# An operation planner on one core: GpSimd left out of the shared work in the first third of the plan, and one weight load moved behind the attention inputs

## The chip, the core and the metric

The kernel runs on one core of a Trainium2 chip. It has the engines TensorE (PE, with its weight loads PEld), VectorE (DVE), ScalarE (ACT), GpSimd (POOL) and SyncE (SP, which here issues the transfers). The metric is the time of one execution on the device in microseconds, as a median of runs. The profile is of one further execution, whose own time stands beside its span below.

## The reference, cut to what matters

Three layers one after the other, on inputs of float32, with weights that arrive as float64 words:

```
for c in range(24):                       # linear attention, chunks of 32 positions
    cum = cumsum(log_a[chunk]);  L = exp(cum_i - cum_j) * causal
    y[chunk] = (C B^T * L) x  +  (C state) * exp(cum)
    state = exp(sum(log_a)) * state + sum_j(B_j x_j * exp(cum_last - cum_j))
xk = mu_k*x + (1-mu_k)*x_prev;  xr = mu_r*x + (1-mu_r)*x_prev     # channel mix
x  = sigmoid(xr @ w_r) * (relu(xk @ w_k)**2 @ w_v)               # 256 -> 1024 -> 256
h  = max(x @ w1, x @ w2, x @ w3);  out = h @ w_out               # 256 -> 768 -> 256
```

Batch 4, 8 heads, 768 positions, head size 32, state 16; 3072 tokens in all.

## The kernel before

The 3072 tokens go through in six tiles t = 0 to 5 of 512 tokens. For each tile the attention makes decay masks, the products of C and B, the chunk states and y; then come the mix, the gate (xr @ w_r), the two feed-forward products and the three-way maximum.

Each float32 operand of a product is split into a high and a low part (names ending in h and l): a copy makes the high part (L414 on ScalarE, L416 on VectorE), and `sub` at L422 subtracts it to leave the low part. A product is then three matmuls (high by high, low by high, high by low). So wkl, wrl, wvl, xk00l, k2l are low parts.

Each weight is loaded by `load_split`: one transfer brings the float64 words as pairs of 32-bit words into a staging buffer (h_93, h_94, woh ...); ScalarE takes the absolute value of the upper words (L630), VectorE turns them into float32 in four steps (L631, L633, L635, L637), and then the copy and the subtraction follow. w_k's first half is loaded in two parts, c = 0 and c = 1 (L659 to L661).

In the attention of a tile, `bd` (L764) is the scaled B for the state update, `sbd` the state (L788 scales it, L790 adds the update `um`), `ce` (L848) the scaled C. TensorE makes the products of C and B in two banks pb (L860), VectorE multiplies them with the masks L (L872), TensorE makes y out of it (L895), which is copied to xb (L933). The mix is L965 to L968, the gate L986, the first feed-forward product L1011 in eight groups f, whose results ScalarE takes out of the banks pa (L1017 ReLU, L1018 square); L1020 and L1021 are the square once more, for the low part.

No order is written by hand. Class `Plan` collects each operation with a cost for each engine that can run it, and a list scheduler places them all, 60 times over with improved keys; the order of the best plan is the order in which the instructions are put onto the engines. An operation that has a cost for "DVE" and one for "POOL" goes to the engine that is free first, in the plan's time (`now`, in ns). In `forward` GpSimd leaves such an operation alone only if VectorE is free or has other work that needs the port which the two engines share in the plan. A key is lowered by the operation's bias; a transfer's bias is `first` plus the plan's bias of the moment. `AHEAD[0]` is the bias of the mix for the feed-forward of tile 0, `AHEAD[1]` the bias in force while w_k's first half is declared, and `FIRST` the bias of the first transfers (b_t 9.85e5, x 9.8e5, c_w 9.9e5, w_r 9.83e5, w_k 9.5e5, mus 9.95e5, c_t 9.6e5; b_t and c_w carry C and B of tile 0).

Of the kernel before, what the change touches and what calls it, by code (L numbers as in the profile page):

```python
# [25 lines left out]
class Ring:  # L26
# [6 lines left out]
    def next(self):  # L33
        b = self.bufs[self.i % len(self.bufs)]
        self.i += 1
        return b
# [39 lines left out]
class Plan:  # L76
# [14 lines left out]
    FIRST = 1500.0  # L91
# [5 lines left out]
    WARM = (3400.0, 430.0, 215.0, 100.0, 200.0)  # L97
    EARLY = 104
    ROUNDS = 60
    SPARE = (200.0, 1000.0)  # L100
    ENGINES = ("PE", "ACT", "POOL", "DVE", "SP")

# [35 lines left out]
    def forward(self, key, spare):  # L138
# [36 lines left out]
        while done < n:  # L175
            now = heapq.heappop(events)
# [15 lines left out]
            for e in self.ENGINES:  # L192
# [12 lines left out]
                if e == "POOL":  # L205
                    if "DVE" in ops[i][0]:
                        mine = next((k for k in sorted(q) if where[k[1]] is None and "DVE" not in ops[k[1]][0]), None)
                        wanted = free["DVE"] <= now or any(
                            ops[k[1]][8] and k[1] != i and where[k[1]] is None for k in ready["DVE"])
                        if wanted:  # L210
                            if mine is None:
                                if free["DVE"] > now:
                                    heapq.heappush(events, free["DVE"] + 1.0)
                                continue
                            q.remove(mine)
                            heapq.heapify(q)
                            heapq.heappush(q, (q[0][0] - 1.0 if q else mine[0], mine[1]))
                elif e == "DVE" and port > now and ops[i][8]:
                    other = min((k for k in q if not ops[k[1]][8] and where[k[1]] is None), default=None)
                    if other is not None:  # L220
                        q.remove(other)
                        heapq.heapify(q)
                        heapq.heappush(q, (q[0][0] - 1.0, other[1]))
# [70 lines left out]
    def arrange(self):  # L294
# [11 lines left out]
        best = None  # L306
        for k in range(self.ROUNDS):
            start, end, where = self.forward(key, self.SPARE[k % len(self.SPARE)])
            if best is None or max(end) < best[0]:
# [27 lines left out]
SPREAD = 2  # L337
LATE = 0
EARLY1 = -20000.0
AHEAD = (60000.0, 60000.0)  # L340
FIRST = (9.85e5, 9.8e5, 9.9e5, 9.83e5, 9.5e5, 9.95e5, 9.6e5)


# [1 line left out]
def kernel(  # L345
# [24 lines left out]
    FF = w_k.shape[1]  # L370
# [74 lines left out]
    b_wk = [[Buf(), Buf()] for _ in range(KC)]  # L445
# [199 lines left out]
    def weights_front():  # L645
        plan.bias = BIAS[2]
        dma(100, mu.rearrange("p i c -> p (i c)"), mus, w=[b_mu], first=FIRST[5])
        op("DVE", 100, lambda: V.tensor_scalar(
            out=om, in0=mu, scalar1=-1.0, scalar2=1.0, op0=ALU.mult, op1=ALU.add), r=[b_mu], w=[b_om])
        fs = [slice(0, FF // 2), slice(FF // 2, FF)]  # L650
        wide, narrow = [Buf(), Buf()], [Buf(), Buf()]
        b_pre.extend(wide[:1] + narrow[:1])
        plan.bias = BIAS[1]
        load_split(w_r.rearrange("p (k n) -> p k n", k=KC), wr_t[0], wr_t[1], KC, CH, [b_wr], FIRST[3],
                   place=(stage.next(2 * TW), word.next(TW)))
        plan.bias = AHEAD[1]
        spots = [(stage.next(2 * TW), word.next(TW)), ((wo_f[0][:, :2 * TW], wide[:1]), word.next(TW)),
                 (stage.next(4 * TW), (wo_f[1][:, :2 * TW], narrow[:1]))]
        for c in range(KC):  # L659
            load_split(w_k[c * P:(c + 1) * P, None, fs[0]], wk_t[0][:, c:c + 1, fs[0]], wk_t[1][:, c:c + 1, fs[0]],  # L660
                       1, FF // 2, [b_wk[c][0]], FIRST[4] - 1.5e5 * c, place=spots[c])  # L661
        plan.bias = 0.0
        k = [begun['loads']]
        load_split(w_k[:, fs[1]].rearrange("(c p) n -> p c n", p=P), wk_t[0][:, :, fs[1]], wk_t[1][:, :, fs[1]],
                       KC, FF // 2, [b_wk[c][1] for c in range(KC)], FIRST[4] - 4e5, place=spots[2], after=k)
        inputs(1, (FIRST[4] - 4.2e5, FIRST[4] - 4.3e5), after=k)
        dma(935, bt.rearrange("p u i -> p (u i)"), b_t[1], w=[b_bt], first=FIRST[4] - 4.4e5, after=k)
        dma(1870, cw.rearrange("p u i -> p (u i)"), c_w[1], w=[b_cw], first=FIRST[4] - 4.5e5, after=k)
        dma(935, ct.rearrange("p u i -> p (u i)"), c_t[1], w=[b_ct], first=FIRST[4] - 2e5)
        for f in range(FC // 4):  # L670
            load_split(w_v[f].rearrange("p (k n) -> p k n", k=4), wv_t[0][:, 4 * f:4 * f + 4], wv_t[1][:, 4 * f:4 * f + 4], 4, CH, [b_wv[f]])
# [323 lines left out]
    def ffn(half, t):  # L995
        hv, cols, bs, n = tokens(half)
        xkt, b_xkt = xk_hl[t % 2], b_xk[t % 2]
        plan.bias += AHEAD[0] * (t == 0)
        mix(0, xkt, b_xkt, half, t)
        plan.bias -= AHEAD[0] * (t == 0)  # L1000

# [125 lines left out]
    plan.switch = begun['spread'], begun['carried']  # L1127
    plan.bias = 0.0
    weights_front()
    sums()  # L1130
    weights_back()
# [93 lines left out]
```

## Time and profile before

| what | value |
| --- | --- |
| time, median of 3 runs | 407.53 us (407.53 to 408.23) |
| time of the profiled execution | 408.05 us |
| its span | 406.3 us |
| PE busy | 396.3 us, 98% |
| DVE busy | 257.9 us, 63% |
| ACT busy | 216.1 us, 53% |
| POOL busy | 55.0 us, 14% |
| granted TensorE clock | 0.9 or more in all 40 slices |

The span runs from the first to the last instruction of the profiled execution. The difference of 1.75 us between its time and its span is start and end around it. Busy shares are over the whole span; what limits a stretch has to be read from that stretch.

### The profile page before, as it was taken

How to read it: one execution, taken by the hardware profiler on the slowest of the kernel's cores; microseconds unless marked ns; L12 is line 12 of the kernel's file. 1: busy time of each engine (PE TensorE's matmuls, PEld its weight loads, DVE VectorE, ACT ScalarE, POOL GpSimd, SP SyncE). 2: the span in 40 equal slices, each digit the busy share in tenths (PEclk: the TensorE clock that was granted, in tenths of full speed). 3: DMA queues.
4: the chain of work that ended last, by engine and by line, in shares of the span. 5: the costliest groups of instructions: out<-in, count | busy, mean ns of one | idle time of the engine just before them, and what ended most of it. 6: DMA issues, size and time to landing. Idle time of an engine off the chain costs nothing.

```text
span 406.3 us, 8667 instructions
## 1 busy us (share of the span) xinstructions
PE 396.3 (98%) x3684; PEld 318.0 (78%) x3684; DVE 257.9 (63%) x417; ACT 216.1 (53%) x379; POOL 55.0 (14%) x60
## 2 busy tenths in 40 slices
PE   8789999999999999999999999999999999999996
PEld 5557877788877888888888888888787888888885
DVE  5898999999998945573735473755373315430632
ACT  6489878954767743355743255753246733321321
POOL 5121000000004100421400231320022200010010
PEclk9999999999999999999999999999999999999999
DMA  7596559541335200206100002300000000001001
GB/s 251 187 369 193 180 139 259 164 141 33 129 112 152 73 26 0 71 38 177 31 27 0 28 2 66 66 26 0 2 2 27 0 26 2 0 0 54 0 2 52
DMA packets 12879, 31.55 MB, mean 78 GB/s; under 512 B 1768, under 2 KB 4136, under 8 KB 12072
## 3 DMA queue, kind: packets, MB, share of 16 engines
q1 hardware_dynamic: 12840, 30.99, 24.7%
q8 instruction: 29, 0.48, 0.5%
q14 instruction: 10, 0.08, 0.1%
HBM read 27.64 MB, written 3.34 MB: 76 GB/s over the span
## 4 chain that ended last, share of the span: by engine, by line
PE 80%; DVE 13%; issue 2%; DMA 2%; ACT 2%; SPq 0%; DVEq 0%; ACTq 0%
PE pa L689 32%; PE pa L1032 14%; PE pa L1011 13%; PE pa L1108 9%; PE pa L986 3%; PE pb L1108 2%; DVE L L872 2%; DVE tmp L1070 1%; PE pb L895 1%; DMA h<-in_w_k_dram 1%; PE pb L860 1%; DVE k2l L422 1%; DMA outs<-in_w_out_dram 1%; DVE tmp L968 1%; DVE h L637 1%
## 5 line engine op out<-in xcount | busy, mean ns | idle before, releaser
L1070 DVE TENSOR_TENSOR tmp<-tmp,pa 128x512 f32<-128x512 f32 x72 | 49.0, 684 | 55.3 <-PE pa L689 54.5
L422 DVE TENSOR_TENSOR k2l<-tmp,k2h 128x512 fp32r<-128x512 f32 x53 | 39.9, 764 | 40.9 <-ACT tmp L1020 34.0
L414 ACT ACTIVATE hr<-tmp 128x512 fp32r<-128x512 f32 x35 | 22.1, 632 | 69.3 <-DVE tmp L1070 69.1
L1032 PE MATMUL pa<-k2h,wvh 128*128 128x512 f32 x96 | 38.2, 398 | 0.0
L1032 PE MATMUL pa<-k2h,wvl 128*128 128x512 f32 x96 | 38.0, 395 | 0.0
L1032 PE MATMUL pa<-k2l,wvh 128*128 128x512 f32 x96 | 37.8, 393 | 0.0
L1108 PE MATMUL pa<-hr,worh 128*128 128x512 f32 x120 | 37.4, 393 | 0.0
L1017 ACT ACTIVATE tmp<-pa 128x512 f32<-128x512 f32 x48 | 28.3, 590 | 10.3 <-PE pa L1011 8.6
L1068 ACT ACTIVATE tmp<-pa 128x512 f32<-128x512 f32 x36 | 21.5, 598 | 21.8 <-PE pa L689 20.2
L1018 ACT ACTIVATE k2h<-tmp 128x512 fp32r<-128x512 f32 x48 | 30.2, 631 | 2.6 <-PE pa L1032 1.0
L422 DVE TENSOR_TENSOR hr<-tmp,hr 128x512 fp32r<-128x512 f32 x28 | 19.5, 700 | 14.8 <-ACT hr L414 14.7
L1108 PEld LDWEIGHTS pa<-hr,worh 128*128 128x128 f32 x120 | 22.3, 188 | 5.3 <-ACT th L991 0.7
L422 POOL TENSOR_TENSOR hr<-tmp,hr 128x512 fp32r<-128x512 f32 x8 | 10.3, 1292 | 110.8 <-ACT hr L414 110.8
L1020 ACT ACTIVATE tmp<-tmp 128x512 f32<-128x512 f32 x37 | 23.2, 630 | 0.8
L1108 PE MATMUL pa<-hr,worl 128*128 128x512 f32 x60 | 23.4, 389 | 0.0
L1032 PEld LDWEIGHTS pa<-k2h,wvh 128*128 128x128 f32 x96 | 18.0, 188 | 4.4 <-ACT k2h L414 0.2
L1032 PEld LDWEIGHTS pa<-k2h,wvl 128*128 128x128 f32 x96 | 18.0, 188 | 4.4
L1032 PEld LDWEIGHTS pa<-k2l,wvh 128*128 128x128 f32 x96 | 18.0, 188 | 4.1
L790 POOL TENSOR_TENSOR sbd<-sbd,um 128x256 f32<-128x256 f32 x2 | 3.1, 1548 | 117.8 <-DVE sbd L788 117.8
L1079 ACT ACTIVATE outs<-pa 128x512 f32<-128x512 f32 x9 | 5.4, 600 | 25.5 <-PE pa L1108 25.5
L968 DVE SCALAR_TENSOR_TENSOR tmp<-xb,bits,tmp 128x512 f32<-128x512 f32 x24 | 17.2, 745 | 0.3
L872 DVE TENSOR_TENSOR L<-pb,L 128x512 f32<-128x512 f32 (+1 forms) x28 | 15.7, 603 | 1.6 <-PE pb L860 0.8
(273 smaller groups left out, 977.4 us busy)
## 6 DMA issues: line engine op xcount, KB each, us to landing
h<-in_w_dram SPq DMA_DIRECT2D x6, 768.0 KB, 5.0
L<-crd SPq DMA_DIRECT2D x8, 512.0 KB, 6.9
cw<-in_c_w_dram SPq DMA_DIRECT2D x6, 512.0 KB, 4.5
xt<-in_x_l_dram SPq DMA_DIRECT2D x6, 512.0 KB, 7.8
out_dram<-outs SPq DMA_DIRECT2D x10, 256.0 KB, 2.0
h<-in_w_v_dram SPq DMA_DIRECT2D x2, 1024.0 KB, 7.6
bt<-in_b_t_dram SPq DMA_DIRECT2D x6, 256.0 KB, 4.7
bl<-in_b_l_dram SPq DMA_DIRECT2D x6, 256.0 KB, 6.5
```

The source lines that it names most:

```text
L414: A.activation(ap(out_), ap(in_), AF.Copy)
L422: op({"DVE": tt(n), "POOL": pool(n, narrow)}, 0, lambda e: (V if e == "DVE" else G).tensor_sub(ap(out_), ap(x0), ap(x1)), r=r, w=w, after= ...
L689: T.matmul(pt, l, r_, start=(i == 0), stop=(i == last))
L872: op("DVE", tt(2 * step * HP), lambda q=q, b=b, lq=lq: V.tensor_mul(lq, W[q].ap[:, b * P:(b + step) * P].rearrange("p (b r i) -> p r b i", ...
L1011: T.matmul(p.ap[:, :n], l, r_, start=(c == 0 and i == 0), stop=(c == KC - 1 and i == 2))
L1017: op("ACT", 51 + 0.833 * n, lambda: A.activation(sq, p.ap[:, :n], AF.Relu), r=[p], w=[tm])
L1018: op("ACT", act(n), lambda: A.activation(hi, sq, AF.Square), r=[tm], w=[kb])
L1020: A.activation(sq, sq, AF.Square) if e == "ACT" else
L1032: T.matmul(pv[c2].ap[:, :n], l, r_, start=(f == 0 and i == 0), stop=(f == FC - 1 and i == 2))
L1068: op("ACT", 51 + 0.833 * TW, lambda p=p, tm=tm: A.activation(tm.ap, p.ap, AF.Copy), r=[p], w=[tm])
L1070: op("DVE", tt(TW), lambda p=p, tm=tm: V.tensor_tensor(out=tm.ap, in0=tm.ap, in1=p.ap, op=ALU.max), r=[p], w=[tm])
L1108: T.matmul(p.ap, l, r_, start=(g == 0 and i == 0), stop=(g == GC - 1 and i == 2))
```

## The change

A class constant `QUIET` of 140000 (plan ns) is added. As long as the plan's time is below it, GpSimd takes no operation that VectorE could run too; it takes one that only it or another engine can run, or nothing. `AHEAD` goes from 60000 to 20000 in both entries: the mix of tile 0 and the steps of w_k's first half get less bias. The transfer of w_k's first half has `AHEAD[1]` taken off its own `first`, so that its whole bias goes from 1.01e6 to 9.5e5 for c = 0, and from 8.6e5 to 8.0e5 for c = 1.

```diff
--- before.py
+++ after.py
@@ -97,6 +97,7 @@
     WARM = (3400.0, 430.0, 215.0, 100.0, 200.0)
     EARLY = 104
     ROUNDS = 60
+    QUIET = 140000.0
     SPARE = (200.0, 1000.0)
     ENGINES = ("PE", "ACT", "POOL", "DVE", "SP")
 
@@ -207,7 +208,7 @@
                         mine = next((k for k in sorted(q) if where[k[1]] is None and "DVE" not in ops[k[1]][0]), None)
                         wanted = free["DVE"] <= now or any(
                             ops[k[1]][8] and k[1] != i and where[k[1]] is None for k in ready["DVE"])
-                        if wanted:
+                        if wanted or now < self.QUIET:
                             if mine is None:
                                 if free["DVE"] > now:
                                     heapq.heappush(events, free["DVE"] + 1.0)
@@ -337,7 +338,7 @@
 SPREAD = 2
 LATE = 0
 EARLY1 = -20000.0
-AHEAD = (60000.0, 60000.0)
+AHEAD = (20000.0, 20000.0)
 FIRST = (9.85e5, 9.8e5, 9.9e5, 9.83e5, 9.5e5, 9.95e5, 9.6e5)
 
 
@@ -658,7 +659,7 @@
                  (stage.next(4 * TW), (wo_f[1][:, :2 * TW], narrow[:1]))]
         for c in range(KC):
             load_split(w_k[c * P:(c + 1) * P, None, fs[0]], wk_t[0][:, c:c + 1, fs[0]], wk_t[1][:, c:c + 1, fs[0]],
-                       1, FF // 2, [b_wk[c][0]], FIRST[4] - 1.5e5 * c, place=spots[c])
+                       1, FF // 2, [b_wk[c][0]], FIRST[4] - AHEAD[1] - 1.5e5 * c, place=spots[c])
         plan.bias = 0.0
         k = [begun['loads']]
         load_split(w_k[:, fs[1]].rearrange("(c p) n -> p c n", p=P), wk_t[0][:, :, fs[1]], wk_t[1][:, :, fs[1]],
```

The line numbers of the changed kernel are one higher from L100 on.

**The transfers at the start.** SyncE issues the transfers in this order behind those of la and mus (h_94 is a staging buffer; `128x1024` is 512 KB, `128x512` 256 KB). Before:

```order
L427 DMA h_94<-in_w_k_dram 128x1024
L427 DMA cw<-in_c_w_dram 128x1024
L427 DMA bt<-in_b_t_dram 128x512
L427 DMA bl<-in_b_l_dram 128x512
L427 DMA h_94<-in_w_r_dram 128x1024
L427 DMA xt_121<-in_x_l_dram 128x1024
```

After:

```order
L428 DMA cw<-in_c_w_dram 128x1024
L428 DMA bt<-in_b_t_dram 128x512
L428 DMA bl<-in_b_l_dram 128x512
L428 DMA h_94<-in_w_r_dram 128x1024
L428 DMA xt_121<-in_x_l_dram 128x1024
L428 DMA ct<-in_c_t_dram 128x512
L428 DMA h_94<-in_w_k_dram 128x1024
L428 DMA woh<-in_w_k_dram 128x1024
```

The transfer of w_k's first part has moved from the third place behind that of ct; cw, bt, bl and w_r each stand 512 KB earlier.

**VectorE at the start.** It begins the weights and the first tile's masks so (rows behind lal, the low part of the log decays; h_92 is the float32 word buffer). Before, w_k's steps, then the eight products with the masks in four lines:

```order
L631 TENSOR_SCALAR h_92<-h_92 128x512
L633 TENSOR_SCALAR h_92<-h_92 128x512
L635 SCALAR_TENSOR_TENSOR h_92<-h_94,h_92 128x512
L598 CAST tri<-h_91 128x128
L637 SCALAR_TENSOR_TENSOR h_92<-h_94,h_92 128x512
L422 TENSOR_TENSOR wkl<-h_92,wkh 128x512
L872 TENSOR_TENSOR L<-pb_135,L 128x2x128 x2
L872 TENSOR_TENSOR L<-pb_136,L 128x2x128 x2
L872 TENSOR_TENSOR L<-pb_135,L 128x2x128 x2
L872 TENSOR_TENSOR L<-pb_136,L 128x2x128 x2
```

After, bd first, and the steps of w_r with its low part among and behind the eight products:

```order
L765 TENSOR_TENSOR bd<-bl,dfj 128x512
L873 TENSOR_TENSOR L<-pb_135,L 128x2x128 x2
L873 TENSOR_TENSOR L<-pb_136,L 128x2x128 x2
L632 TENSOR_SCALAR h_92<-h_92 128x512
L634 TENSOR_SCALAR h_92<-h_92 128x512
L636 SCALAR_TENSOR_TENSOR h_92<-h_94,h_92 128x512
L873 TENSOR_TENSOR L<-pb_135,L 128x2x128 x2
L873 TENSOR_TENSOR L<-pb_136,L 128x2x128 x2
L638 SCALAR_TENSOR_TENSOR h_92<-h_94,h_92 128x512
L632 TENSOR_SCALAR h_92<-h_92 128x512
L634 TENSOR_SCALAR h_92<-h_92 128x512
L423 TENSOR_TENSOR wrl<-h_92,wrh 128x512
```

The steps of w_k come behind those of w_r, and its low part wkl, which stood ahead of the eight products, comes eight rows after this piece.

**GpSimd behind its set-up.** L573 is the last of the constants. Before:

```order
L573 TENSOR_TENSOR bits<-um 128x2
L764 TENSOR_TENSOR bd<-bl,dfj 128x512
L788 TENSOR_TENSOR sbd<-sbd,ec 128x256
L422 TENSOR_TENSOR wrl<-h_92,wrh 128x512
L764 TENSOR_TENSOR bd<-bl,dfj 128x512
L422 TENSOR_TENSOR k2l_100<-tmp_107,k2h_99 128x512
L790 TENSOR_TENSOR sbd<-sbd,um 128x256
L1021 TENSOR_TENSOR tmp_110<-tmp_110 128x512
L1021 TENSOR_TENSOR tmp_107<-tmp_107 128x512
L422 TENSOR_TENSOR L<-L,ccol 128x512
L790 TENSOR_TENSOR sbd<-sbd,um 128x256
```

After:

```order
L574 TENSOR_TENSOR bits<-um 128x2
L791 TENSOR_TENSOR sbd<-sbd,um 128x256
L849 TENSOR_TENSOR ce<-ct,ec 128x512
L423 TENSOR_TENSOR hr_1444<-tmp_109,hr_1444 128x512
L928 COPY xb_129<-xb_130 128x8
```

Nine operations are gone from GpSimd here, among them L788 sbd and the two L1021. VectorE goes from 399 to 406 rows (ScalarE and VectorE also exchange some).

**ScalarE at w_v.** The rows around the second half of w_v (wd<-h_93 is its absolute value, wvh the high part of the first half; pa_131 and pa_132 are TensorE's banks). Before:

```order
L1018 ACTIVATE k2h_103<-tmp_109 128x512
L1020 ACTIVATE tmp_109<-tmp_109 128x512
L1017 ACTIVATE tmp_110<-pa_132 128x512
L414 ACTIVATE wvh<-h_92 128x1024
L1017 ACTIVATE tmp_107<-pa_131 128x512
L1018 ACTIVATE k2h_105<-tmp_110 128x512
L630 ACTIVATE wd<-h_93 128x1024
```

After:

```order
L1021 ACTIVATE tmp_109<-tmp_109 128x512
L1018 ACTIVATE tmp_110<-pa_132 128x512
L631 ACTIVATE wd<-h_93 128x1024
L415 ACTIVATE wvh<-h_92 128x1024
L1018 ACTIVATE tmp_107<-pa_131 128x512
L1019 ACTIVATE k2h_105<-tmp_110 128x512
L1021 ACTIVATE tmp_110<-tmp_110 128x512
```

The absolute value of w_v's second half has moved ahead of wvh, and so ahead of the ReLU that empties the bank pa_131.

## Rows read from the trace of the kernel before

**Rows 1.** Busy time of each engine in two stretches (us; clock, DMA share, GB/s last)

```profile
24.00:64.00 40.00, 39.09 (x600) 30.04 (x600) 38.66 (x54) 33.40 (x61) 3.25 (x2) 1.00 0.66 212
64.00:126.00 62.00, 61.55 (x625) 49.35 (x625) 61.51 (x113) 43.30 (x81) 0.00 (x0) 1.00 0.43 125
```

**Rows 2.** What TensorE waited for after 24 us (total, times, longest)

```profile
PE pb L727 <- issue: 1.5, 1, 1.5
PE pa L1011 <- ACT tmp L1017: 0.8, 1, 0.8
PE pa L1011 <- DVE outs L1081: 0.4, 1, 0.4
```

**Rows 3.** The end of the chain of waits from 36 to 64 us

```profile
62.41 0.61 DVE xk00l L422
...
63.75 0.50 PE pa L1011
```

**Rows 4.** GpSimd's timeline, 9 to 36 us (start, duration, what)

```profile
9.79 1.06 POOL L764 TENSOR_TENSOR bd<-bl,dfj 128x512 f32<-128x512 f32 x1 [3.23 <-DMA bl<-in_b_l_dram]
...
19.61 1.27 POOL L422 TENSOR_TENSOR wrl<-h,wrh 128x512 fp32r<-128x512 f32 x1 [4.06 <-ACT wrh L414]
24.24 1.53 POOL L764 TENSOR_TENSOR bd<-bl,dfj 128x512 f32<-128x512 f32 x1 [3.36 <-DMA bl<-in_b_l_dram]
32.90 1.73 POOL L422 TENSOR_TENSOR k2l<-tmp,k2h 128x512 fp32r<-128x512 f32 x1 [7.13 <-DVE wol L635]
```

**Rows 5.** VectorE's timeline, 0 to 70 us

```profile
6.91 0.43 DVE L631 TENSOR_SCALAR h<-h 128x512 f32<-128x512 f32 x1 [0.41 <-ACT h L630]
...
7.83 0.69 DVE L635 SCALAR_TENSOR_TENSOR h<-h,h 128x512 uint32<-128x512 uint32 x1
...
9.96 1.44 DVE L422 TENSOR_TENSOR wkl<-h,wkh 128x512 fp32r<-128x512 f32 x1 [0.70 <-ACT wkh L414]
...
12.55 2.08 DVE L872 TENSOR_TENSOR L<-pb,L 128x256 f32<-128x256 f32 x6 [0.82 <-PE pb L860]
15.45 0.42 DVE L872 TENSOR_TENSOR L<-pb,L 128x256 f32<-128x256 f32 x1 [0.82 <-PE pb L895]
...
19.99 1.44 DVE L637 SCALAR_TENSOR_TENSOR wd<-woh,wd 128x512 uint32<-128x512 uint32 x1
...
24.16 2.16 DVE L422 TENSOR_TENSOR k2l<-tmp,k2h 128x512 fp32r<-128x512 f32 x2 [0.34 <-ACT k2h L414]
...
31.05 0.69 DVE L631 TENSOR_SCALAR h<-h 128x1024 f32<-128x1024 f32 x1 [0.60 <-ACT h L630]
...
33.40 2.32 DVE L637 SCALAR_TENSOR_TENSOR wol<-h,wol 128x1024 uint32<-128x1024 uint32 x1
...
37.73 1.22 DVE L422 TENSOR_TENSOR wkl<-wol,wkh 128x1024 fp32r<-128x1024 f32 x1 [0.55 <-ACT wkh L414]
...
55.10 1.28 DVE L422 TENSOR_TENSOR k2l<-tmp,k2h 128x512 fp32r<-128x512 f32 x2
```

**Rows 6.** ScalarE's timeline, 0 to 45 us

```profile
10.92 0.67 ACT L630 ACTIVATE h<-h 128x512 f32<-128x512 f32 x1 [0.51 <-DMA h<-in_w_r_dram]
...
41.22 0.59 ACT L1017 ACTIVATE tmp<-pa 128x512 f32<-128x512 f32 x1
...
42.21 1.15 ACT L630 ACTIVATE wd<-h 128x1024 f32<-128x1024 f32 x1
```

**Rows 7.** TensorE's timeline, 0 to 45 us

```profile
9.13 0.70 PE L860 MATMUL pb<-cw,bt 32*64 32x128 f32 x32 [0.56 <-DMA bt<-in_b_t_dram]
...
26.15 0.58 PE L986 MATMUL pa<-k2h,wrh 128*128 128x512 f32 x1
```

**Rows 8.** Issues of w_v's two halves (KB, us from issue to landing)

```profile
h<-in_w_v_dram SPq DMA_DIRECT2D x1, 1024.0 KB, 10.4
...
h<-in_w_v_dram SPq DMA_DIRECT2D x1, 1024.0 KB, 4.9
```

**Rows 9.** Busy time in the first stretch after 126 us

```profile
126.00:140.00 14.00, 14.00 (x61) 11.43 (x62) 12.17 (x22) 11.57 (x22) 5.62 (x4) 1.00 0.59 151
```

## The prediction

> **What bounds the kernel now.** I read the busy times by stretch first, since the shares over the whole span hide the stages. From 24 to 64 us VectorE is busy 38.66 of 40 us and TensorE 39.09; from 64 to 126 us it is 61.51 and 61.55 of 62 [rows 1]. Two engines are full at once, so the waits have to say which one leads. Behind 24 us TensorE waits for anything but its own queue in only three places: 1.5 us for its own issue (while it makes the second tile's masks), 0.8 us for a ReLU of ScalarE, and 0.4 us for an eviction by VectorE [rows 2]. The chain followed back from that ReLU ends in xk00l, a low part that VectorE has done at 63.0 us, and TensorE goes on at 63.75 [rows 3]; the steps ahead of it on that chain are nearly all VectorE's. So up to 63 us VectorE's queue decides when TensorE goes on, and behind it TensorE runs to the end without a gap except for the 0.4 us. What the change is worth is what it does to the time at which VectorE ends xk00l, plus that 0.4 us. I place three landmarks on VectorE: the last of the eight products with the masks ends at 15.87 us (15.45 + 0.42), the second low part of the gate's operand ends at 26.32 (24.16 + 2.16), xk00l at 63.0 [rows 3, 5]. The gate's first matmul starts at 26.15, within the second of these [rows 7].
>
> **GpSimd's operations, taken back.** The early five are bd, sbd, wrl, bd, k2l. An operation with two operands costs VectorE one step of 0.60 us at 512 elements (two of them take 1.28 us, where one shows 0.69) and about 0.34 at 256 (six take 2.08, one 0.42) [rows 5]. So they cost it 4 x 0.60 + 0.34 = 2.74 us. But they held it up where they were. Each long VectorE row here began while a GpSimd row ran, and ended about 0.6 us (1.2 at 1024 elements) after that one's end: wkl 1.44 us from 9.96 beside bd 9.79 to 10.85; L637 1.44 from 19.99 beside wrl 19.61 to 20.88; two k2l 2.16 from 24.16 beside bd 24.24 to 25.77; L637 2.32 from 33.40 beside k2l 32.90 to 34.63 [rows 4, 5]. Against 0.69, 0.69, 1.28 and 1.22 without company [rows 5] that is 0.75 + 0.75 + 0.88 + 1.10 = 3.48 us of standstill. Taken back, the five are therefore worth only 0.7 us in VectorE's favour; the rest of the gain has to come from the order.
>
> The Trainium skill, SBUF — State Buffer, section "Who interferes with whom", says that VectorE and GpSimd share a port pair under an exclusive lock, held for the whole instruction, the loser standing fully blocked, also for a VectorE operation with two SBUF inputs against a GpSimd one that reads SBUF. The rows agree: wkl ends 0.55 us after bd, as if it had started there. By that rule the four standstills go in full; by a rule of shared bandwidth part of them would stay, but the rows show no such part.
>
> **The front, up to 15.87 us.** The transfers land in the order of issue: bl at 9.79 (GpSimd was waiting for it), w_r at 10.92 (ScalarE was) [rows 4, 6]. In the new order the same bytes stand ahead of and in w_r as now in and ahead of bl (512 + 256 + 256 KB, and w_r's 512 in place of w_k's). So w_r should land near 9.7. ScalarE's step takes 0.67, so 10.35; VectorE's three steps 1.61 (from 6.91 to 8.52) [rows 5], so 11.95; the last four products with the masks stand behind them, 4 x 0.34, so 13.3. The bank they read has been made by then: the first products of C and B started at 9.13, waiting for bt [rows 7], which comes 512 KB earlier. bd is VectorE's first such step (0.60) and hides in the wait for w_r. If w_r lands no earlier than now, it is 10.92 + 0.67 + 1.61 + 1.36 = 14.55; if nothing in the front comes earlier, 15.87.
>
> **From there to the gate.** Now 26.32 − 15.87 = 10.45 us. Two standstills lie in it and go (0.75 + 0.88). Work changes: the four steps of w_k, wrl and wkl come in (0.34 + 0.34 + 4 x 0.60 = 3.08), three steps of w_r and one of w_k's second part go out (0.34 + 0.34 + 2 x 0.60 = 1.88): +1.20. This gives 10.0 and a landmark of 23.3 (24.6 and 25.9 for the two worse fronts). TensorE could start its gate earlier than that, so it is again VectorE that it meets.
>
> **From the gate to xk00l.** Now 63.0 − 26.3 = 36.7 us. The standstill of 1.10 goes. VectorE gets more in this piece: L637 that moved behind (0.60), sbd (0.34), a copy to the high part and a masked update from ScalarE (0.34 each), bd and k2l (0.60 each), a weight's low part of 768 elements drawn ahead of xk00l (0.87, priced by the difference of the 512 and 1024 steps), less a copy that went to ScalarE (0.60): +3.09. One idle time of 0.60, in which VectorE waits for ScalarE's step on w_v's first half at 31.05 [rows 5], goes at least in part because VectorE now comes to it later in its own list: that half took 10.4 us to land [rows 8], and its issue hangs on buffers that come free earlier, not later. I take it as gone; the other idle time of 0.55 at 37.73 I leave, since its cause is ScalarE's order. So 36.7 − 1.1 + 3.1 − 0.6 = 38.1, and xk00l is done at 61.4. TensorE follows 0.75 behind, as now: 62.15 against 63.75, −1.6 us. With 24.6 it is −0.3, with 25.9 it is +1.0.
>
> **Behind it.** The low part of 0.87 us is no longer in the 62 us that follow, and the eviction that TensorE waits for (0.4) goes to ScalarE: −0.4 us, with nothing as the other bound. The last four of the nine operations (sbd and three of 0.60, 2.1 us) come to VectorE behind 126 us, where it is busy 12.17 of 14 us [rows 9] in the fullest stretch, and TensorE does not wait. I cost them at nothing; were the cover gone, 0.6 us for each that stands at the head of a wait.
>
> **The sum.** −1.6 − 0.4 = −2.0 us on the profiled 408.05, 406.05. The median of the runs lies 0.5 below the profiled time, so 405.5. About 0.2%, 0.8 us, is what a measurement of this kernel can tell from no change.
>
> **The rivals.** (1) The front gains little: w_r lands no earlier than now, because the transfers share what the memory gives rather than their order. Then −0.3 and −0.4 give 406.8; if the front gains nothing at all +1.0 − 0.4 gives 408.1. For it speaks that the landing times above are worked out, not seen; against it that bt, bl and w_r landed in order and that engines waited for two of them [rows 4, 7].
>
> (2) Slower: w_v's second half lands late. Its absolute value (1.15 us, now at 42.21) stands ahead of wvh and of the ReLU that empties pa_131 (now 41.22 to 41.81) [rows 6]. ScalarE takes its list in order, so the ReLU waits for the transfer, and TensorE for the bank. The transfer can be issued when VectorE has read the buffer with L637 (33.40, end 35.72), in the new order near 31.6. With the 4.9 us that it took [rows 8] it lands at 36.5 and costs nothing. It decides from 40.9 on. With the 10.4 us of the first half it lands at 42.0, the ReLU ends at 42.0 + 1.15 + 1.05 (wvh) + 0.6 = 44.8, 3.0 us later than now; less the 0.8 that TensorE waits later anyway, and the 0.4: +1.8, so 409.3. For it speaks that the same size did take 10.4 us once, against it that the queue was then behind much else.
>
> (3) More gain: the idle time of 0.55 goes as well, and the front gains the 0.6 us by which the landings are uncertain. xk00l at 60.2, then −2.8 − 0.4 gives 404.3.
>
> (4) GpSimd's work runs beside VectorE's almost freely, the long rows being late for other reasons. Then three of the standstills that I take off behind the front (0.75 + 0.88 + 1.10 = 2.73 us) stay: 405.5 + 2.7 gives 408.2. The rows speak against it, four times out of four. The Trainium skill, Perfetto Trace Analysis, section "Optimizing Scalar/DVE Operations", says that with VectorE saturated some of its work may well go to GpSimd, which speaks against this change, and adds that the shared port may undo it.
>
> **How the numbers follow.** My forecast 0.52, with 404.6 to 406.5 of its own; rival 1 0.20, rival 2 0.12, rival 3 0.12, rival 4 0.04. Faster by over 0.2% are the forecast and rival 3: 0.64. Within it rivals 1 and 4: 0.24. Slower rival 2: 0.12. The range goes from rival 3's lower side, 404.0, to rival 4 and the worse half of rival 1, 408.2; it leaves out rival 2.
>
> **What the new profile would show.** Right: no GpSimd row with two operands ahead of 126 us, and no subtraction of 512 elements on VectorE above 0.7 us nor one of 1024 above 1.25; the last product with the masks ends near 13.3, the gate's second low part near 23.3, xk00l near 61.4; TensorE restarts near 62.2 and shows short waits between 23 and 62 us that add up to two or three, since its work from the gate on is less than VectorE's. The step that fails is the front if w_r's absolute value starts at 10.9 or behind, the piece from the gate if VectorE shows idle times for ScalarE's copies, and rival 2 if VectorE is well ahead while the ReLU behind w_v's absolute value ends behind 42 us. The prediction is wrong if VectorE is done at 61.4 and TensorE still goes on at 63.75, since something else then holds it.

## The result: slower by 0.6 per cent, and the profile after

The changed kernel takes 410.63 us as a median of 20 runs (407.3 to 413.5), the kernel before 407.53 (20 runs, 407.1 to 410.0): a ratio of 1.0058, 95% interval 1.0037 to 1.0078. A second set gave 410.22 against 407.91, again 1.0058 (1.0032 to 1.0085). I had forecast 405.5. The profiled execution took 411.31 us with a span of 409.6, 3.3 more than before.

Busy time by stretch, as in [rows 1] (the columns are PE, PEld, DVE, ACT, POOL, the granted clock, DMA share, GB/s):

```profile
0.00:24.00 24.00, 20.59 (x502) 13.91 (x502) 17.30 (x40) 15.34 (x31) 4.68 (x24) 1.00 0.62 220
24.00:64.00 40.00, 36.07 (x569) 27.70 (x570) 38.39 (x59) 30.44 (x53) 0.00 (x0) 1.00 0.70 229
64.00:126.00 62.00, 60.02 (x617) 48.00 (x616) 59.70 (x108) 44.54 (x83) 0.00 (x0) 1.00 0.41 121
```

The kernel before, up to 24 us:

```profile
0.00:24.00 24.00, 18.80 (x479) 13.11 (x480) 17.94 (x38) 15.44 (x28) 8.34 (x27) 1.00 0.69 243
```

Up to 24 us TensorE is busy 20.59 us, 1.8 more than the 18.80 of before: the front did gain. From 24 to 64 it loses 3.0 (36.07 against 39.09), from 64 to 126 another 1.5. What it waited for behind 24 us, to be held against [rows 2]:

```profile
PE pa L1012 <- ACT tmp L1018: 4.3, 3, 2.3
PE pa L1012 <- DVE wkl L423: 0.7, 1, 0.7
PE pb L896 <- issue: 0.7, 1, 0.7
PE pa L987 <- DVE k2l L423: 0.5, 1, 0.5
```

4.3 us are for ReLUs of ScalarE (L1018 here is L1017 of before), in three pieces. ScalarE's timeline at the two large ones answers to [rows 6]:

```profile
38.39 0.61 ACT L1018 ACTIVATE tmp<-pa 128x512 f32<-128x512 f32 x1
41.05 1.12 ACT L631 ACTIVATE wd<-h 128x1024 f32<-128x1024 f32 x1 [2.05 <-DMA h<-in_w_v_dram]
42.06 1.05 ACT L415 ACTIVATE wvh<-h 128x1024 fp32r<-128x1024 f32 x1
43.01 0.59 ACT L1018 ACTIVATE tmp<-pa 128x512 f32<-128x512 f32 x1
...
65.09 0.89 ACT L631 ACTIVATE h<-h 128x768 f32<-128x768 f32 x1 [3.77 <-DMA h<-in_w_dram]
65.88 0.62 ACT L415 ACTIVATE xk01h<-tmp 128x512 fp32r<-128x512 f32 x1
66.40 0.58 ACT L1018 ACTIVATE tmp<-pa 128x512 f32<-128x512 f32 x1
```

At the first place ScalarE is idle 2.05 us for the landing of w_v's second half, and the ReLU of group 4 stands two rows behind the waiting one, at 43.01 (41.22 before). At the second it is idle 3.77 us for the next weight (768 columns), and behind that row stand xk01h and the second tile's first ReLU, at 66.40. Before, the same row stood behind the second tile's first two ReLUs (L1017) and found the weight landed:

```profile
63.10 0.60 ACT L1017 ACTIVATE tmp<-pa 128x512 f32<-128x512 f32 x1 [0.50 <-DVE xk00l L422]
...
64.26 0.58 ACT L1017 ACTIVATE tmp<-pa 128x512 f32<-128x512 f32 x1
64.93 0.92 ACT L630 ACTIVATE h<-h 128x768 f32<-128x768 f32 x1
```

In the changed kernel TensorE starts again right behind each of the two late ReLUs:

```profile
43.65 0.50 PE L1012 MATMUL pa<-xk00h,wkh 128*128 128x512 f32 x1 [2.31 <-ACT tmp L1018]
...
67.03 0.50 PE L1012 MATMUL pa<-xk10h,wkh 128*128 128x512 f32 x1 [1.82 <-ACT tmp L1018]
```

67.03 is the start that stood at 63.75 before [rows 3]: 3.28 us later, as much as the span grew. VectorE, answering to [rows 5]:

```profile
9.44 0.69 DVE L765 TENSOR_TENSOR bd<-bl,dfj 128x512 f32<-128x512 f32 x1 [2.58 <-DMA bl<-in_b_l_dram]
...
14.14 1.09 DVE L873 TENSOR_TENSOR L<-pb,L 128x256 f32<-128x256 f32 x3 [0.82 <-PE pb L896]
...
20.55 0.68 DVE L423 TENSOR_TENSOR wkl<-h,wkh 128x512 fp32r<-128x512 f32 x1
...
23.53 1.28 DVE L423 TENSOR_TENSOR k2l<-tmp,k2h 128x512 fp32r<-128x512 f32 x2
...
42.20 0.69 DVE L632 TENSOR_SCALAR wd<-wd 128x1024 f32<-128x1024 f32 x1 [1.14 <-ACT wd L631]
...
63.23 0.69 DVE L423 TENSOR_TENSOR xk00l<-tmp,xk00h 128x512 fp32r<-128x512 f32 x1
...
66.53 0.69 DVE L423 TENSOR_TENSOR xk01l<-tmp,xk01h 128x512 fp32r<-128x512 f32 x1 [1.74 <-ACT xk01h L415]
```

No row waits for GpSimd any more (0.68 for wkl, 1.28 for two k2l), the second k2l ends at 24.81 (26.32 before), but xk00l only at 63.92, 0.9 later than before, after 1.14 us of idle time behind w_v's second half. The issues of the two transfers, as in [rows 8]:

```profile
h<-in_w_v_dram SPq DMA_DIRECT2D x1, 1024.0 KB, 7.7
```

```profile
h<-in_w_dram SPq DMA_DIRECT2D x1, 768.0 KB, 7.1
```

### The profile page after: what moved, and what is told of

Read it like the earlier page. It is cut to its first block, busy times and chain, and to the rows that moved or that the text cites. A ratio compares the mean times of both kernels' runs of the same rounds, so it can differ in the third digit from the quotient of the medians.

```text
span 409.6 us, 8659 instructions
## 1 busy us (share of the span) xinstructions
PE 396.8 (97%) x3683; PEld 317.5 (78%) x3683; DVE 258.5 (63%) x427; ACT 214.2 (52%) x377; POOL 42.1 (10%) x51
## 4 chain that ended last, share of the span: by engine, by line
PE 85%; DMA 8%; ACT 2%; DVE 2%; issue 1%; SPq 1%; ACTq 0%; DVEq 0%
PE pa L690 36%; PE pa L1033 15%; PE pa L1012 13%; PE pa L1109 10%; DMA h<-in_w_v_dram 4%; PE pa L987 3%; PE pb L1109 2%; PE pb L896 2%; DMA h<-in_w_dram 2%; DMA bl<-in_b_l_dram 2%; PE pb L886 1%; PE pb L861 1%; SPq L428 1%; PE pb L774 1%; DVE L L873 1%
## 5 line engine op out<-in xcount | busy, mean ns | idle before, releaser
L423 DVE TENSOR_TENSOR k2l<-tmp,k2h 128x512 fp32r<-128x512 f32 x54 | 38.9, 730 | 39.9 <-ACT tmp L1021 33.3
L1018 ACT ACTIVATE tmp<-pa 128x512 f32<-128x512 f32 x48 | 28.2, 590 | 9.7 <-PE pa L1012 9.5
L1021 ACT ACTIVATE tmp<-tmp 128x512 f32<-128x512 f32 x37 | 23.3, 632 | 0.8
L1080 ACT ACTIVATE outs<-pa 128x512 f32<-128x512 f32 x10 | 6.0, 597 | 24.8 <-PE pa L1109 24.8
L791 POOL TENSOR_TENSOR sbd<-sbd,um 128x256 f32<-128x256 f32 x1 | 1.1, 1052 | 161.4 <-DVE sbd L789 161.4
```

Of the source, the lines that this page charges most:

```text
L423: op({"DVE": tt(n), "POOL": pool(n, narrow)}, 0, lambda e: (V if e == "DVE" else G).tensor_sub(ap(out_), ap(x0), ap(x1)), r=r, w=w, after= ...
L1018: op("ACT", 51 + 0.833 * n, lambda: A.activation(sq, p.ap[:, :n], AF.Relu), r=[p], w=[tm])
L1021: A.activation(sq, sq, AF.Square) if e == "ACT" else
```

## The experiments

Theory A: ScalarE takes its list in order (in the rows above it ran nothing while it stood 2.05 and 3.77 us for a landing), so a row that waits for a transfer at its head holds the ReLUs behind it, and TensorE's banks with them. Rivals: B, the transfers are late in any order; C, the work that VectorE took over is the cause; later D, the transfers are slow because they share the queue. Most experiments move single rows of the finished plan and leave every other row of every engine where it was. The diffs are cut to the lines that set the order. Each ratio is against runs of the kernel before on the same chip.

| run | median, us | ratio, 95% interval |
| --- | --- | --- |
| changed kernel again | 410.22 | 1.0058 (1.0032 to 1.0085) |
| both places moved | 409.63 | 1.0033 (1.0016 to 1.0050) |
| first place moved | 410.69 | 1.0060 (1.0036 to 1.0084) |
| second place moved | 408.14 | 0.9996 (0.9977 to 1.0015) |
| before, first place made early | 409.18 | 1.0030 (1.0012 to 1.0049) |
| before, second place made early | 409.34 | 1.0035 (1.0015 to 1.0055) |
| before, five operations to VectorE | 407.99 | 0.9989 (0.9964 to 1.0015) |
| GpSimd's rule alone | 408.92 | 1.0029 (1.0009 to 1.0048) |
| bias and w_k's transfer alone | 412.87 | 1.0089 (1.0048 to 1.0129) |
| transfers held back | 412.26 | 1.0094 (1.0071 to 1.0117) |
| three moves | 408.31 | 1.0005 (0.9978 to 1.0032) |
| three moves and bd | 408.72 | 1.0019 (1.0005 to 1.0033) |
| six moves | 411.08 | 1.0070 (1.0044 to 1.0096) |
| second place and three rows | 412.34 | 1.0107 (1.0077 to 1.0136) |
| second place, and ec's transfer behind w_v's | 408.31 | 1.0007 (0.9987 to 1.0027) |

**The changed kernel again.** 

> The changed kernel itself, for comparison on this chip: 2 to 3.5 us over before, with runs spread over some 5 us. What its profile shows is read with the earlier one: a wait of 1 to 3 us near 43 and one of 1 to 3 us near 66, both behind a transfer's reader in ScalarE's list.

Its profile has waits of 1.99 us at 43.00 and 1.20 at 66.39, as expected. Here w_r landed sooner, so that its front is the one I forecast:

```profile
8.69 1.42 DVE L873 TENSOR_TENSOR L<-pb,L 128x256 f32<-128x256 f32 x4 [1.22 <-PE pb L861]
...
12.81 1.09 DVE L873 TENSOR_TENSOR L<-pb,L 128x256 f32<-128x256 f32 x3 [0.81 <-PE pb L896]
...
22.20 1.29 DVE L423 TENSOR_TENSOR k2l<-tmp,k2h 128x512 fp32r<-128x512 f32 x2
```

The products with the masks end at 13.90, the second k2l at 23.49, and the span is 408.9 all the same: what the front gives is taken at the two places, and in this execution by TensorE's clock as well, which was granted at 0.96 from 24 to 64 us (0.50 from 44 to 47 us, right behind the wait of 1.99):

```profile
24.00:64.00 40.00, 36.31 (x566) 27.86 (x565) 36.97 (x56) 30.31 (x53) 0.00 (x0) 0.96 0.68 226
```

**Both places, and each alone.** The edit places the plan's start of the row behind that of a ReLU (abs 5 is the absolute value of w_v's second half, abs 8 that of the next weight):

```diff
+def adjust(self):   # called at the start of issue()
+    for a, b in [(('abs', 5), ('relu', 0, 4)), (('abs', 8), ('relu', 1, 1))]:
+        i, j = self.tags[a], self.tags[b]
+        at = self.start[i] = self.start[j] + 0.1
+        # ... (users of the row that would stand ahead of it go along)
```

> The changed kernel with two instructions of ScalarE put later in its own list and nothing else: the absolute value of w_v's second half goes behind the ReLU of group 4, and the absolute value of the next weight (768 columns) goes behind the ReLU of the second tile's group 1. Theory A (two instructions that wait for a transfer at the head of ScalarE's list hold the ReLUs behind them, TensorE's 2.31 us at 43.65 and 1.82 us at 67.03): both waits fall under 0.5 us. The first alone is worth little in the end, because VectorE's low parts for the next tile (xk10l, xk11l, ended at 61.85) then bind; the second is worth its 1.8: time 1.4 to 2.4 us under the changed kernel's 410.6, so 408.2 to 409.2. Theory B (the transfers are late, so whatever needs them is late, in any order): within 0.4 us of 410.6. Theory C (VectorE's added work is the cause alone): within 0.4 us of 410.6, and the waits only change their releaser to VectorE.

The first pair alone:

> The changed kernel with the first of the two moves alone (w_v's second half behind the ReLU of group 4). Theory A: the wait of 2.31 us at 43.65 falls under 0.5, the wait of 1.8 us near 67 stays, since the next weight lands near 65 as before, and the time stays within 0.4 us of 410.6. Theory B: the wait at 43.65 stays above 1.5 us. Theory C: as A for the time, with a VectorE releaser at 43.

The second alone:

> The changed kernel with the second move alone (the next weight's absolute value behind the ReLU of the second tile's group 1). Theory A: the wait of 1.82 us at 67.03 goes, that of 2.31 at 43.65 stays, and the time falls by 1.5 to 2.0 us, to 408.6 to 409.1. Theory B: no change over 0.4 us. Theory C: no change over 0.4 us, with the wait at 67 now on VectorE.

The second place is worth the whole deficit: 1.0058 falls to 0.9996, some 2.5 us, more than the 1.5 to 2.0 expected (about 1.5 us among runs at a granted clock of 0.998 or more, see the last section), and the start that stood at 67.03 comes at 63.47 (67.28 is that of the fifth group, two later):

```profile
42.45 0.50 PE L1012 MATMUL pa<-xk00h,wkh 128*128 128x512 f32 x1 [1.96 <-ACT tmp L1018]
...
63.47 0.50 PE L1012 MATMUL pa<-xk10h,wkh 128*128 128x512 f32 x1
...
67.28 0.51 PE L1012 MATMUL pa<-xk10h,wkh 128*128 128x512 f32 x1 [0.34 <-ACT tmp L1018]
```

B falls with that, and C as the sole cause, since neither the order of the transfers nor VectorE's list changed. The first place moved alone leaves the time where it was, as A had it, but that run does not price the place: the wait at 43.65 is gone, and TensorE stands for wvl instead.

```profile
44.69 0.50 PE L1033 MATMUL pa<-k2h,wvl 128*128 128x512 f32 x1 [1.69 <-DVE wvl L423]
```

The wait at the second place, which was to stay at 1.8 us, was 0.90 in that profile. With both moved the time is 1.5 us worse than with the second alone, which A had not foreseen: the wait for the transfer went from ScalarE's list to VectorE's, where two steps of w_v's second half stand ahead of wvl.

```profile
42.05 0.69 DVE L632 TENSOR_SCALAR wd<-wd 128x1024 f32<-128x1024 f32 x1 [1.64 <-ACT wd L631]
```

```profile
44.86 0.50 PE L1033 MATMUL pa<-k2h,wvl 128*128 128x512 f32 x1 [1.92 <-DVE wvl L423]
```

**The same places in the kernel before.** The reverse edits:

```diff
+    for a, b in [(('abs', 5), ('relu', 0, 3))]:             # first place
+        i, j = self.tags[a], self.tags['relu', 1, 0]        # second place: abs 8
+        at = self.start[i] = self.start[j] + 500.0
```

> The kernel before with one instruction of ScalarE put earlier: the absolute value of w_v's second half stands ahead of wvh and of the ReLU of group 4, as in the changed kernel. Theory A: the transfer lands at 40.6, so the ReLU ends near 40.7 + 1.15 + 1.05 + 0.6 = 43.5 instead of 41.8, TensorE waits 1.3 to 1.7 us near 42, of which the 0.77 us that it waits later are taken off: 0.4 to 1.0 us over the kernel before, 408.0 to 408.5. Theory B: no change over 0.3 us. Theory C: no change over 0.3 us, since VectorE's work is the same.

> The kernel before with one instruction of ScalarE put earlier: the absolute value of the next weight (768 columns, landing at 64.9 us) stands between the second tile's ReLUs of groups 0 and 1 instead of behind that of group 1. It is the second place of the changed kernel in a milder form. Theory A: the ReLU of group 1 ends near 64.9 + 0.9 + 0.6 + 0.6 = 67.0 instead of 64.8 with the square's row between, TensorE waits 1 to 2 us near 65 to 67, nothing gives it back: 1.0 to 2.0 us over before, 409.1 to 410.1. Theory B (readers of late transfers cost the same in any order): no change over 0.4 us.

Measured 1.0 us (0.3%) and 1.5 us (0.35%) over before, each with the wait that theory A names, 1.52 us and 1.77 us:

```profile
45.96 0.50 PE L1011 MATMUL pa<-xk00h,wkh 128*128 128x512 f32 x1 [1.52 <-ACT tmp L1017]
```

```profile
66.64 0.50 PE L1011 MATMUL pa<-xk10h,wkh 128*128 128x512 f32 x1 [1.77 <-ACT tmp L1017]
```

The first is a little above the 0.4 to 1.0 us expected. In its profiled execution TensorE's clock was granted at 0.50 from 12 to 24 us and what followed came later, so its wait stands at 45.96 and not near 42. One row moved by two or three positions makes the kernel before slower by a third of a per cent, with VectorE's and GpSimd's work untouched.

**The price of GpSimd's operations.** In the plan of before, five operations change engine at their place:

```diff
+        if self.where[i] == "POOL" and "DVE" in o[0] and 5000.0 < self.start[i] < 60000.0:
+            self.where[i] = "DVE"
```

> The kernel before, every instruction where it was, but the five early operations of GpSimd (bd, sbd, wrl, bd, k2l) run on VectorE at the same place of the order. It prices the first half of the change without any reordering. By my step (five operations cost VectorE 2.74 us and take 3.48 us of standstill away) the long rows beside GpSimd shrink to 0.69, 0.69, 1.28 and 1.22 us, and the time is 0.4 to 1.0 us under the kernel before: 407.1 to 407.7 on a chip with before at 408.1. Rival, GpSimd ran beside VectorE nearly for free: 1.5 to 2.7 us over before, 409.6 to 410.8, and the rows stay long for another reason.

The interval holds no change, so the time alone does not decide; the rows do. All four long rows of [rows 5] shrink to their price (wkl, wd, two k2l, the 1024-wide step):

```profile
10.79 0.68 DVE L422 TENSOR_TENSOR wkl<-h,wkh 128x512 fp32r<-128x512 f32 x1
...
20.52 0.68 DVE L637 SCALAR_TENSOR_TENSOR wd<-woh,wd 128x512 uint32<-128x512 uint32 x1
...
25.17 1.29 DVE L422 TENSOR_TENSOR k2l<-tmp,k2h 128x512 fp32r<-128x512 f32 x2 [0.98 <-ACT k2h L414]
...
34.27 1.22 DVE L637 SCALAR_TENSOR_TENSOR wol<-h,wol 128x1024 uint32<-128x1024 uint32 x1
...
61.74 0.68 DVE L422 TENSOR_TENSOR xk00l<-tmp,xk00h 128x512 fp32r<-128x512 f32 x1
```

xk00l ends at 62.42 instead of 63.0 and TensorE restarts at 63.17 instead of 63.75, 0.6 us, where I had priced 0.7. That is one execution against one, and the clock fell in this one from 14 to 18 us, so the 0.6 is a rough figure. The Trainium skill, SBUF — State Buffer, section "Who interferes with whom", calls the shared port pair an exclusive lock and has the loser fully blocked; with GpSimd's rows gone the four standstills (0.75, 0.75, 0.88 and 1.10 us) go in full, which agrees.

**Each half of the change, planned anew.**

```diff
+    QUIET = 140000.0   # first run: this and its test alone
-AHEAD = (60000.0, 60000.0)   # second run: this and `- AHEAD[1]` alone
+AHEAD = (20000.0, 20000.0)
```

> The changed rule for GpSimd alone, the bias and the transfer of w_k's first half as before, planned anew. In this order the next weight's absolute value stands behind the second tile's first two ReLUs, and that of w_v's second half behind wvh and the ReLU of group 3, but ahead of the ReLU of group 4. Theory A (the place of the transfers' readers in ScalarE's list decides): no wait near 65 and at most 1.5 us near 42, so 0 to 1 us over before: 408.1 to 409.1. Theory C (the operations that VectorE takes over are the cause): as the changed kernel, 2 to 3 us over before.

> The bias and the moved transfer of w_k's first half alone, GpSimd's rule as before, planned anew. Here too the next weight's absolute value stands behind the second tile's ReLUs, while that of w_v's second half stands ahead of wvh and the ReLU of group 4. Theory A: a wait of 1 to 2 us near 42, none near 65, so 0 to 1 us over before: 408.1 to 409.1. Theory C: no change against before or faster, since VectorE's work is as before.

The first came in the range of A, at +0.3%, its upper end. But its profile has no wait of TensorE near 42 or 65 us, so by it A explains none of the 0.3%; what does stays open. The second did not come in the range: 412.87 lies 3.8 us above the 409.1 that A allowed at most, and above the whole change. Its profiled execution shows the wait of A at the first place (1.89 us at 42.76) and 0.88 at 68.98, but that execution took 410.3 us; the runs went from 409.1 to 415.6. The three runs with a mean granted clock of 1.00 took 409.1 to 409.3 us, about A's upper bound; the six at 0.990 to 0.992 took 410.3 to 415.6. So what lies above A's range comes with a lower clock, shown in the last section; why runs at the same mean clock differ by 5 us stays open.

**Is it the queue?** Transfers issued later (numbers of the plan's operations; bl, cw, bt of the third tile, and L):

```diff
+    for i, at in ((412, 37500.0), (385, 37510.0), (384, 37520.0), (388, 62600.0), (389, 62610.0)):
+        self.start[i] = at
```

> The changed kernel with two groups of transfers issued later and nothing else: bl, cw and bt of the third tile go behind the load of the next weight, and the two transfers of L behind the load after that. Theory D (w_v's second half took 7.7 us and the next weight 7.1 because they share the queue with those): both land 2 to 3 us sooner, at 38 to 39 and at 62 to 63.5, the two waits of TensorE fall under 0.7 us, and the time falls by 1.5 to 2.5 us, to about 0 to 1 us over before. Theory A alone (the order on ScalarE, with the landing given by what went before): the landings move by less than 1 us and the time by less than 0.5 us.

Half a miss. The next weight was there at 62.43 (65.09 in the changed kernel), as D had it, and TensorE's wait at the second place went; w_v's half still took 7.3 us. And the time rose by 2.0 us, to 412.26. A later weight's load, issued at 69.88, now stood behind the two of L and one of ec, issued 2.6 to 3.8 us ahead of it, and took 9.8 us, with its reader at the head of ScalarE's list again, and TensorE then waited 1.36 us for a k2l at 81.94; that this is the whole 2.0 us was not tried.

```profile
79.76 0.89 ACT L631 ACTIVATE h<-h 128x768 f32<-128x768 f32 x1 [4.22 <-DMA h<-in_w_dram]
```

What w_v's half stands behind is the transfer of ec, issued 1.9 us ahead of it (4.5 before). With the second place mended as above:

```diff
+    at = self.start[122] + 0.1    # 122: the transfer of w_v's second half
+    self.start[274] = at          # 274: that of ec
```

> The changed kernel with the second move on ScalarE (the next weight's absolute value late, the run that was level with before), and the transfer of ec issued behind w_v's second half instead of ahead of it. If ec's transfer is what w_v's half stands behind: w_v's half takes 4.5 to 5.5 us instead of 6.5 to 7.7 and lands by 38.5, TensorE's wait of 2.0 us near 42.5 falls under 0.7, and the time is 0.3 to 1.5 us under that run, 0.1 to 0.4 per cent under before. If the landing is set by something else: w_v's half lands at 39.5 to 41 as in the others and the time is within 0.4 us of before.

The half was issued at 33.23 and had landed when ScalarE came to it at 38.70, without waiting, and TensorE's wait fell from 1.96 to 0.36:

```profile
38.70 1.17 ACT L631 ACTIVATE wd<-h 128x1024 f32<-128x1024 f32 x1
```

```profile
41.35 0.50 PE L1012 MATMUL pa<-xk00h,wkh 128*128 128x512 f32 x1 [0.36 <-ACT tmp L1018]
```

Ahead of ec the half took 5.5 us at most; behind it, with the second move alone, it took 6.9. The Trainium skill, DMA: Bandwidth & Descriptors, section "Queues, rings and completion order", says that all that SyncE issues goes through one ring on each DMA engine, consumed in order; the run agrees. The time did not move (1.0007 against 0.9996): in this order the first place costs nothing.

**The rest of the forecast gain.** Three moves: both of the first experiment, and on VectorE the two steps behind wvl.

```diff
+    for d, i in enumerate((124, 125)):
+        at = self.start[121] + 0.1 * (d + 1)
+        self.start[i] = at
```

> The changed kernel with the two moves on ScalarE and a third on VectorE: the first two steps of w_v's second half go behind wvl. In the run with the two moves alone VectorE stood 1.6 us before those steps, and TensorE then 1.9 us for wvl. Theory A, widened to every engine that takes its list in order: without the third place the wait near 43 falls under 0.6 us, VectorE's idle time of 1.6 goes, and the time is 0.5 to 1.5 us under the run with the second move alone (which was level with before), so 0.1 to 0.4 per cent under before. Rival (VectorE's work is the bound and its idle time only moves): level with the run with the two moves alone, 0.3 per cent over before.

The waits went as A said (VectorE no longer stands before those steps, and TensorE not for wvl), the time did not: level with before and with the second move alone, between what either theory expected. Then bd behind the first four products:

```diff
+    self.start[36] = 9941.0
```

> The three moves, and bd, which stands ahead of the first four products with the masks on VectorE and waits there for bl until 9.4 us, put behind those four. By my reading of the front the first four products start near 7.7 instead of 10.05, TensorE's idle time of 1.0 us at 9.8 goes, and the last of the eight products ends 0.7 to 1.7 us sooner than 15.2. If VectorE's work then sets the end, the time is 0.3 to 1.2 us under the three moves; if the transfers' landing sets it, no change over 0.3 us.

The products started at 7.99, ended at 14.03, and the time stayed. Against the three moves, where they ended at 14.24, the end came only 0.2 us sooner, so little was won for the time to show. Last, three more rows behind xk01l and the ReLUs:

```diff
+    for a, b in [(('abs', 5), ('relu', 0, 4)), (('abs', 8), ('relu', 1, 2))]:
+    # ... (as in the first experiment, and the third move)
+    for i, at in ((147, self.start[273] + 0.1), (152, self.start[273] + 0.2), (313, self.start[self.tags['relu', 1, 1]] + 0.1)):
+        self.start[i] = at
```

> The changed kernel with the three moves (w_v's second half behind the ReLU of group 4 and, on VectorE, behind wvl; the next weight's absolute value late) and three more rows later: on VectorE wg0l and one weight step behind xk01l, on ScalarE the square of the second tile's group 0 behind the ReLU of group 1, and the next weight's absolute value behind the ReLU of group 2. If the order of these rows takes what the front gave: xk00l ends 0.8 us sooner than 62.4, the third group of the second tile starts at 62.2 to 62.6 instead of 63.2, the fifth at 65.2 to 66.0 instead of 67.0, and the time is 0.8 to 1.6 us under the three moves, 0.2 to 0.4 per cent under before. If VectorE's and ScalarE's total work up to there sets the pace, no change over 0.3 us against the three moves.

> The same without the moves at the first place: w_v's second half stands at the head of ScalarE's list near 40 us as in the changed kernel. If the first place costs something of its own, it is 0.5 to 2.0 us slower than e11_six; if VectorE's work behind it takes up that wait, it is within 0.3 us of it.

A clear miss: with all six moves 2.7 us slower than with three (1.0070 against 1.0005), and slower again without the first place's (1.0107; the intervals overlap, so its price in this order is not settled). xk00l ended at 62.41, as with three moves and not 0.8 us sooner. The rows I put later were what others waited for: wg1h now waits 0.96 us for VectorE's last step at the head of ScalarE's list, the absolute value comes behind it, and VectorE stands 1.84 us for that, with a k2l behind.

```profile
65.97 0.84 ACT L415 ACTIVATE wg1h<-wd 128x768 fp32r<-128x768 f32 x1 [0.96 <-DVE wd L638]
...
67.20 0.88 ACT L631 ACTIVATE h<-h 128x768 f32<-128x768 f32 x1
```

```profile
68.11 0.56 DVE L632 TENSOR_SCALAR h<-h 128x768 f32<-128x768 f32 x1 [1.84 <-ACT h L631]
```

No version beats the kernel before by more than its interval; the lowest ratio is that of the five operations on VectorE.

## Why the prediction was wrong, point by point

- **What bounds the kernel:** right up to 63 us for the kernel before, but incomplete. I took VectorE's end of xk00l, and TensorE 0.75 us behind it, as the only landmark. In the changed kernel xk00l ended at 63.92 and TensorE went on at 67.03, 3.1 behind, because the ReLU between them stood behind a transfer's reader. This step failed ("TensorE follows 0.75 behind, as now"), and it is the whole loss against the kernel before: the move of that one row gave 2.5 us back. It is about half of the miss against the forecast, by the profiles: TensorE went on 4.9 us later than the 62.15 I had worked out, 2.4 by this step and 2.5 because xk00l itself ended at 63.92 and not at 61.4 (1.5 up to the gate, 1.0 behind it). I had seen the same danger at w_v, and called it rival 2 with 0.12; I did not look for other readers that had moved forward in ScalarE's list, and the one that decided was 24 us further on.
- **Rival 2** named the mechanism, at the place where it costs nothing in this order: its wait came (2.31 us, landing at 41.0, so past its point of 40.9), yet with the second place mended, taking it away moved the time by nothing (three moves 1.0005, ec's transfer 1.0007, against 0.9996). VectorE's work up to xk00l takes it up: with ec's transfer moved, xk00l ended at 62.39 and TensorE restarted at 63.67, against 62.72 and 63.47. In the kernel before, the same wait did cost 1.0 us.
- **GpSimd's operations taken back:** right as to the standstills, which went in full (the pair of k2l began 0.08 us ahead of bd, not while it ran as I wrote); 0.6 against 0.7 us in one profile, while the runs (0.9989, 0.9964 to 1.0015) cannot tell it from nothing.
- **The front:** right where w_r lands in time. The second k2l was forecast at 23.3; it ended at 23.3 to 23.9 in nine profiles of this front, at 24.8 where w_r was there only at 10.63, and at 24.6 in one more. That it came out so near is partly luck: the piece from the products to the gate took 9.6 us (13.85 to 23.43 with the second place moved) against 10.0, and the products with the masks end 0.4 to 0.9 late, since I let the last four follow each other although a row of [rows 5] showed VectorE waiting 0.82 us for TensorE between them.
- **From the gate to xk00l:** too short by 1.0 us. With the second place mended, and nothing else in VectorE's way, xk00l ended at 62.4 to 62.7 against 61.4. There VectorE stands 0.3 to 0.5 us each for xk00h and xk01h, at 25 and 27 us, which I had not priced; I had only taken an idle time away. In the changed kernel's first profile the idle times were others, 0.36 us for bl at 35.16 and the 1.14 behind w_v's second half.
- **Behind it:** the 1.6 us that were to come at the restart shrank, with the second place mended, to 0.1 to 0.6 (63.2 to 63.7 against 63.75), and two groups later nothing was left (67.0 to 67.3 against 66.6). My try to win it back by moving three rows failed, so where exactly it goes in that order stays open.

## What to carry to other kernels

When a change reorders a list, go through each row of an in-order engine that waits for a transfer, in the new order: which rows stand behind it, who waits for those, and whether the landing as measured, not as planned, comes first. Time won earlier is worth little ahead of such a row where the landing does not move as far: between the two profiles of the changed kernel the gate came 1.3 us sooner, and the two landings only 0.7 (41.05 to 40.40, 65.09 to 64.43). And a wait moved off one engine's list can stand at the head of another's, so a mend is followed through every list that the operand passes.

## What the runs showed of the hardware

A transfer's landing can trail the bulk of the data: in the run with transfers held back the DMA engines moved 393 GB/s from 36 to 37 us, 107, 25 and 33 in the next three, with busy shares of 0.28, 0.06 and 0.09 (0.06 of 16 engines is about one), and only 7.3 us after its issue at 33.0 was w_v's half there, which ScalarE took at 40.37. SyncE issued nothing between the half and 40.17. Whether the slow rest belonged to the half or to ec ahead of it, these shares do not tell.

TensorE's clock fell in some executions. In the run with the bias alone TensorE waited 2.2 us for VectorE and was busy 0.16 of 2 us from 10 to 12; from 14 us it ran at the lower of its two levels, 1.2 GHz (granted 0.50), for some 7 us:

```profile
10.00:12.00 2.00, 0.16 (x9) 0.16 (x16) 1.52 (x4) 1.17 (x3) 0.00 (x0) 1.00 1.02 385
12.00:14.00 2.00, 1.79 (x128) 1.46 (x123) 1.35 (x3) 0.75 (x3) 0.00 (x0) 0.99 0.37 143
14.00:16.00 2.00, 2.00 (x22) 1.78 (x9) 1.90 (x5) 0.44 (x1) 0.00 (x0) 0.50 0.00 0
...
20.00:22.00 2.00, 2.00 (x10) 1.34 (x8) 2.00 (x5) 2.00 (x5) 0.00 (x0) 0.80 1.00 330
22.00:24.00 2.00, 2.00 (x69) 1.43 (x69) 1.89 (x4) 2.00 (x5) 0.00 (x0) 1.00 0.97 367
```

It fell at the first place too. In the changed kernel's second profile it was granted at 0.50 from 44 to 47 us, behind the wait of 1.99, and a matmul of the same shape took 0.63 us where it took 0.39 before; in the run with both places moved it was at 0.50 from 46 to 49, behind the wait of 1.92. Behind like waits in the changed kernel's first profile (2.31) and with the second place moved (1.96) it stayed at 1.00.

Of the changed kernel's twelve runs of the second set, six had a mean granted clock of 0.998 or more, with a median of 409.26 us, and six less, with 411.37. So some of its spread, and perhaps 1 us of its median, is the clock; that shorter waits would end it was not tried. Among runs at 0.998 or more the changed kernel is 1.8 us over the kernel before (409.26 against 407.49), and with the second place moved 0.2 us (408.07 against 407.83). So that one row is worth about 1.5 us without the clock, by six and nine runs; the rest of the 2.5 us would then be the clock's.
